# Attention and two MLPs on one core: transfers counted at 270 GB/s in a planner, softmax normalisation of two blocks also on ScalarE, table changes by rank

## The chip, the cores and the metric

The kernel runs on one core of a Trainium2 chip. The metric is device microseconds of one execution. Engines carry the names of the profile: PE is TensorE, PEld its weight loads, DVE is VectorE, ACT is ScalarE, POOL is GpSimd, SP is SyncE, whose instructions only issue DMAs here.

## What is computed

Chunked attention (4 sequences, 8 heads, 768 tokens, head size 64; chunks of 32 queries see 16 keys to the left, 8 to the right and 8 memory tokens), then two MLPs over the 3072 tokens (512 to 2048 to 512). The weights are 64-bit floats in memory.

```python
def _attn_ref(q, k, v, mem_k, mem_v):
    chunk, left_ctx, right_ctx = (32, 16, 8)
    scale = 1.0 / np.sqrt(D)
    for c in range(S // chunk):
        c_start, c_end = c * chunk, c * chunk + chunk
        l_start, r_end = max(0, c_start - left_ctx), min(S, c_end + right_ctx)
        k_full = np.concatenate([mem_k, k[:, :, l_start:r_end]], axis=2)
        v_full = np.concatenate([mem_v, v[:, :, l_start:r_end]], axis=2)
        scores = scale * np.matmul(q[:, :, c_start:c_end], k_full.transpose(0, 1, 3, 2))
        a = np.exp(scores - np.max(scores, axis=-1, keepdims=True))
        a = a / (np.sum(a, axis=-1, keepdims=True) + 1e-09)
        out[:, :, c_start:c_end] = np.matmul(a, v_full)

# x: the attention's output as 3072 rows of 512
h = x @ w_in;  x = (h * np.tanh(np.log1p(np.exp(h)))) @ w_out        # first MLP (Mish)
h = x @ w2_in; x = (h * (1.0 / (1.0 + np.exp(-1.702 * h)))) @ w2_out  # second MLP
```

## The kernel before

**Tiles and stages.** The tokens are cut into 8 blocks of 384. Each block needs 8 quads of attention (a quad is two heads by 192 tokens) and 16 steps of the first MLP (a step is one slice of 128 of the 2048 hidden columns). The second MLP follows over pairs of blocks, in 32 units with seven products each. Matmuls with fp32 accuracy are made of three in fp32r: a value is split into a rounded part (xh, gh) and a remainder (xl, gl). The attention of block 0 runs alone at the start, that of block j+1 between the steps of block j, so the quads of block 1 lie among the steps of block 0.

**One quad.** For blocks 0 and 1 the heads are turned on PE (L673, bank `h`) and copied out of PSUM by ACT (L680) or DVE (L681) into qT or kT. Scores run on PE (L708, banks s0, s1 and, in block 0, o0, o1), DVE takes the row minimum with the mask (L721), ACT takes the exponentials e and their sums sm (L736, four pieces), DVE makes the sums' reciprocals r (L754, L758) and multiplies e by them (L761). PE turns e (L782), ACT or DVE copies it into aT (L788, L789), PE multiplies by the values vt (L799 in block 0, L808 behind it), and ACT or DVE rounds the result into xh (L834, L836; two halves in blocks 1 and on), DVE makes xl (L840).

**One step.** PE runs twelve matmuls into a bank `h` (L895), ACT applies Mish (L907, into buffers gh and gl in turn in block 0), PE multiplies by the output weights into four banks that are held through the block (L924), which leave through ACT (L951) or DVE (L954). There are two banks `h`, shared by the turning of heads and the steps: a step can't begin before the copy L680 or L681 has emptied its bank.

**Weights.** In block 0 each step's weights are loaded as words of 64 bits (wi, wo, 512 KB each, L299) and made into fp32 by one scaling on ACT or DVE (L343, L346) and three operations on DVE (L352, L356, L360), then split (L378 on ACT or L379 on DVE, L384); those of wo are stored to DRAM for later (w1d).

**What sets the order.** Every piece of work is an operation with a rank (its place in an ideal order; a quad takes 2 ranks, a step 1) and one or more ways, each an engine with an estimated duration. `Plan.issue()` plays these through once when the program is built: whenever an engine is free, it takes the ready operation of the lowest rank. A second way is taken if its engine would be ready sooner than the queue of the first. ACT needs a table for exponentials and another for Mish, and an operation of the other table is taken only if nothing else is ready. A transfer is issued by SP in that order and is thought to land after the transfers before it, at a rate that `bus()` gives, plus a lag. The outcome is a fixed order of instructions on each engine, in which every one waits for its data in place. A planner's number therefore never changes how long an instruction takes; it changes which instruction stands in front of which.

`load` hands each transfer to SP with that time:

```python
size = bus(nbytes / len(parts), run)
ways = [("sp", 0.475, lambda go=go: go(nc.sync), size), ...]
```

Of the kernel before, what the change touches and what calls it, by code (L numbers as in the profile page):

```python
# [81 lines left out]
class Plan:  # L82
# [2 lines left out]

    LAG = {"pe": 0.2, "act": 0.16, "dve": 0.13, "pool": 0.2}
    RELOAD = 1.4

    def __init__(self):
        self.ops = []  # L90

    def add(self, rank, ways, reads=(), writes=(), updates=(), chain=None, table=None):
        op = Op()
        op.table = table
        op.rank, op.ways, op.seq = rank, ways, len(self.ops)
        op.after, op.at = [], 0.0
        need = {}

        def wait(o, lag=True):
            need[id(o)] = (o, lag or need.get(id(o), (o, False))[1])  # L100

        for b in (*reads, *updates):
            for o in b.writers:
                wait(o)
        for b in (*writes, *updates):
            for o in b.readers:
                wait(o)
            b = b.whole
            if not b.users and b.tag is not None:
                made = b.tag.made  # L110
                k = made.index(b)
                if k >= b.tag.bufs:
                    b.gate += [(o, True) for o in made[k - b.tag.bufs].users]
                    made[k - b.tag.bufs].closed = True
                if k:
                    b.gate.append((made[k - 1].users[0], False))
        for b in writes:
            for o, lag in b.whole.gate:
                wait(o, lag)
        for b in updates:  # L120
            b.writers, b.readers = [], []
        for b in (*writes, *updates):
            b.writers.append(op)
        for b in reads:
            b.readers.append(op)
        for b in (*reads, *writes, *updates):
            assert not b.whole.closed
            b.whole.users.append(op)
        if chain is not None:
            if chain:  # L130
                wait(chain[-1], False)
            chain.append(op)
        op.need = len(need)
        for o, lag in need.values():
            o.after.append((op, lag))
        self.ops.append(op)
        return op

    def issue(self):
        engines = ("pe", "act", "dve", "pool", "sp")  # L140
        free = dict.fromkeys(engines, 0.0)
        ready = {e: [] for e in engines}
        load = dict.fromkeys(engines, 0.0)
        coming = []
        bus = 0.0
        for op in self.ops:
            if op.need == 0:
                heapq.heappush(coming, (0.0, op.seq, op))
            op.start = None
        left = len(self.ops)  # L150
        now = 0.0
        table = None
        order = []
        while left:
            while coming and coming[0][0] <= now + 1e-9:
                op = heapq.heappop(coming)[2]
                for w, (e, dur, *_) in enumerate(op.ways):
                    heapq.heappush(ready[e], (op.rank, op.seq, w, op))
                load[op.ways[0][0]] += op.ways[0][1]
            for e in engines:  # L160
                if free[e] > now + 1e-9:
                    continue
                kept = []
                pick = other = None
                while ready[e]:
                    item = heapq.heappop(ready[e])
                    op, w = item[3], item[2]
                    if op.start is not None:
                        continue
                    if w:  # L170

                        e0, d0 = op.ways[0][:2]
                        if max(free[e0] - now, 0.0) + load[e0] - d0 < op.ways[w][1] - d0 + 0.3:
                            kept.append(item)
                            continue
                    if e == "act" and op.table not in (None, table):

                        if other is None:
                            other = item
                        else:  # L180
                            kept.append(item)
                        continue
                    pick = item
                    break
                if pick is None:
                    pick = other
                elif other is not None:
                    kept.append(other)
                for item in kept:
                    heapq.heappush(ready[e], item)  # L190
                if pick is None:
                    continue
                op, w = pick[3], pick[2]
                e_, dur, fn, *size = op.ways[w]
                op.start, op.way = now, w
                load[op.ways[0][0]] -= op.ways[0][1]
                order.append(op)
                left -= 1
                end = now + dur
                if e == "act" and op.table not in (None, table):  # L200
                    if table is not None:
                        end += self.RELOAD
                    table = op.table
                free[e] = end
                lag = self.LAG.get(e, 0.0)
                if size:
                    bus = max(bus, end + 0.65) + size[0]
                    end, lag = bus, 0.9
                for o, far in op.after:
                    t = end + lag if far else (now + 0.01 if not size else now + 0.01)  # L210
                    o.at = max(o.at, t)
                    o.need -= 1
                    if o.need == 0:
                        heapq.heappush(coming, (o.at, o.seq, o))
            times = [coming[0][0]] if coming else []
            times += [free[e] for e in engines if free[e] > now + 1e-9]
            if not times:
                assert not left, "operations wait for one another"
                break
            now = min(t for t in times if t > now) if any(t > now for t in times) else now  # L220
        order.sort(key=lambda o: (o.start, o.seq))
        for op in order:
            op.ways[op.way][2]()


def dve(n, fast=False):
    return (170 + (0.53 if fast else 1.04) * n) / 1000


def act(n, psum=False):  # L230
    return ((180 if psum else 220) + 0.86 * n) / 1000


def bus(nbytes, run):
    return nbytes / 360e3 * (1 if run >= 512 else 2)


@with_exitstack
def kernel(
# [449 lines left out]
    def quad(j, hp, gp, heads, rank):  # L689
# [74 lines left out]

        add(rank + 1.4, [("dve", 0.23, plus)], reads=[sm], writes=[r])
        add(rank + 1.4, [("dve", 0.16, inverse)], updates=[r])
        add(rank + 1.4, [("dve", dve(4 * P), norm)], reads=[r, done], updates=[e])

        return after, e

# [484 lines left out]
```

## Time and profile before

| | us |
|---|---|
| median of 3 runs | 1215.35 (1214.6 to 1215.85) |
| the profiled execution's own time | 1215.45 |
| its span, first to last instruction | 1213.3 |
| PE busy in the span | 1183.9 (98%) |
| DVE busy | 822.5 (68%) |
| ACT busy | 564.9 (47%) |
| POOL busy | 10.1 (1%) |

The profile is of one execution. Its span is 2.15 us shorter than its own time, which holds the launch as well, and its own time is 0.1 us above the median of the runs. The busy time of an engine is the sum of its instructions; an engine that waits in place for data is idle in it. Matmuls are pipelined, and a busy PE can run at either of two levels of its clock, which the profile gives as the granted share of full speed.

### The profile page before, as it was taken

How to read it: one execution, taken by the hardware profiler on the slowest of the kernel's cores; microseconds unless marked ns; L12 is line 12 of the kernel's file. 1: busy time of each engine (PE TensorE's matmuls, PEld its weight loads, DVE VectorE, ACT ScalarE, POOL GpSimd, SP SyncE). 2: the span in 40 equal slices, each digit the busy share in tenths (PEclk: the TensorE clock that was granted, in tenths of full speed). 3: DMA queues.
4: the chain of work that ended last, by engine and by line, in shares of the span. 5: the costliest groups of instructions: out<-in, count | busy, mean ns of one | idle time of the engine just before them, and what ended most of it. 6: DMA issues, size and time to landing. Idle time of an engine off the chain costs nothing.

```text
span 1213.3 us, 19142 instructions
## 1 busy us (share of the span) xinstructions
PE 1183.9 (98%) x6656; PEld 1082.8 (89%) x6656; DVE 822.5 (68%) x2379; ACT 564.9 (47%) x1303; POOL 10.1 (1%) x27
## 2 busy tenths in 40 slices
PE   7689999999999999999999999999999999999998
PEld 6567789999999999999999998998889888988897
DVE  5798878776866767667665668877655855555554
ACT  4677666655555555655533344445212521232112
POOL 1000000000000000000000000000000000000000
PEclk8799999999999999999999999999999999999999
DMA  9965545533433333334212676699656865566521
GB/s 204 262 216 168 147 124 139 147 94 80 114 88 92 98 91 93 103 81 116 60 49 74 229 257 209 231 356 335 214 186 194 296 226 189 179 224 214 181 106 53
DMA packets 214687, 197.80 MB, mean 163 GB/s; under 512 B 133496, under 2 KB 176519, under 8 KB 214591
## 3 DMA queue, kind: packets, MB, share of 16 engines
q1 hardware_dynamic: 214239, 195.82, 53.0%
q0 software_dynamic: 352, 0.75, 0.4%
q8 instruction: 53, 0.87, 0.3%
q14 instruction: 43, 0.35, 0.1%
HBM read 148.29 MB, written 48.23 MB: 162 GB/s over the span
## 4 chain that ended last, share of the span: by engine, by line
PE 93%; DMA 3%; SPq 2%; DVE 1%; ACT 1%; issue 0%; ACTq 0%
PE h L895 22%; PE o L924 22%; PE h L1057 19%; PE o L1084 15%; PE s L1084 7%; PE s L808 3%; PE s L708 3%; SPq L299 2%; PE s L782 2%; DMA vt<-in_v_dram 1%; DMA wo<-in_moe_w_out_dram 0%; DMA wi<-in_q_dram 0%; DMA x1d<-ev 0%; DMA st<-w1d 0%; DMA w1d<-u 0%
## 5 line engine op out<-in xcount | busy, mean ns | idle before, releaser
L895 PE MATMUL h<-xh,wi 128*128 128x384 f32 x1024 | 269.0, 344 | 5.9 <-ACT qT L680 4.4
L924 PE MATMUL o<-gh,wo 128*128 128x384 f32 x896 | 240.6, 349 | 0.0
L895 PEld LDWEIGHTS h<-xh,wi 128*128 128x128 f32 x1024 | 184.3, 189 | 13.2 <-ACT qT L680 5.2
L895 PE MATMUL h<-xl,wi 128*128 128x384 f32 x512 | 172.9, 338 | 0.0
L924 PEld LDWEIGHTS o<-gh,wo 128*128 128x128 f32 x896 | 158.0, 188 | 2.8
L924 PE MATMUL o<-gl,wo 128*128 128x384 f32 x448 | 150.8, 337 | 0.0
L907 ACT ACTIVATE u<-h 128x384 f32<-128x384 f32 x112 | 55.0, 491 | 132.0 <-PE h L895 125.5
L736 ACT ACTIVATE e<-e,mx 96x128 f32<-96x128 f32 x240 | 94.0, 393 | 23.5 <-DVE mx L721 22.9
L944 DVE TENSOR_TENSOR gl<-u,gh 128x384 fp32r<-128x384 f32 x177 | 96.9, 554 | 11.4 <-ACT gh L939 8.6
L895 PEld LDWEIGHTS h<-xl,wi 128*128 128x128 f32 x512 | 96.7, 189 | 0.0
L1057 PE MATMUL h<-wi,wi 128*128 128x384 f32 x480 | 94.4, 337 | 0.0
L1057 PEld LDWEIGHTS h<-wi,wi 128*128 128x128 f32 x480 | 85.5, 188 | 4.9 <-ACT v L1124 0.2
L924 PEld LDWEIGHTS o<-gl,wo 128*128 128x128 f32 x448 | 84.1, 188 | 0.0
L1124 ACT ACTIVATE v<-h 128x384 f32<-128x384 f32 x61 | 29.9, 490 | 113.2 <-PE h L1057 113.2
L1084 PE MATMUL o<-wo,gh 128*128 128x512 f32 x262 | 82.1, 394 | 0.2 <-ACT ev L951 0.2
L721 DVE CUSTOM_DVE_ANT_0 e<-s,mask 96x128 f32<-96x128 f32 x240 | 55.7, 283 | 37.5 <-PE s L708 36.4
L1057 PE MATMUL h<-wo,wi 128*128 128x384 f32 x384 | 77.2, 336 | 0.0
L907 ACT ACT_TABLE_LOAD x55 | 70.6, 1283 | 10.6 <-PE h L895 9.9
L1107 ACT ACTIVATE u<-e 128x384 f32<-128x384 f32 x64 | 33.5, 524 | 85.2 <-DVE e L1130 85.1
L736 ACT ACT_TABLE_LOAD x54 | 69.3, 1283 | 6.7 <-DVE mx L721 5.8
L1057 PEld LDWEIGHTS h<-wo,wi 128*128 128x128 f32 x384 | 68.2, 188 | 3.0 <-DVE u L1109 0.2
L836 DVE CAST xh<-s 64x192 fp32r<-64x192 f32 x84 | 29.8, 355 | 50.9 <-PE s L808 41.6
(195 smaller groups left out, 2057.8 us busy)
## 6 DMA issues: line engine op xcount, KB each, us to landing
wi<-w2c SPq DMA_DIRECT2D x72, 512.0 KB
wo<-w2o SPq DMA_DIRECT2D x48, 512.0 KB
w2c<-wi SPq DMA_DIRECT2D x24, 512.0 KB
st<-x1d SPq DMA_DIRECT2D x56, 192.0 KB
wi<-in_moe_w_in_dram SPq DMA_DIRECT2D x16, 512.0 KB
wo<-in_moe_w_out_dram SPq DMA_DIRECT2D x16, 512.0 KB
st<-in_moe_w_in_dram SPq DMA_DIRECT2D x16, 512.0 KB
w2d<-v SPq DMA_DIRECT2D x32, 256.0 KB
```

Source lines behind the costliest of these rows:

```text
L708: nc.tensor.matmul(out=s[hh][:, i, :], lhsT=queries(d, i), rhs=keys(d, i), start=True, stop=True,)
L721: nc.vector.tensor_tensor_reduce(out=e[:, i, hh, :], in0=s[hh][:, i, :], in1=mask[:GQ, mask_of(g0 + i), :], scale=-scale, scalar=-NEG, op0 ...
L736: nc.scalar.activation(out=e[:, i, hh, :], in_=e[:, i, hh, :], func=AF.Exp, scale=-1.0, bias=mx[:, i, hh:hh + 1], accum_out=sm[:, i, hh:hh ...
L808: nc.tensor.matmul(out=o[:, i].rearrange("p h t -> p (h t)"), lhsT=vt[:, g + i, h:h + 2].rearrange("p h d -> p (h d)"), rhs=aT[:, i].rearr ...
L895: nc.tensor.matmul(out=h.get(), lhsT=a[:, c], rhs=b[:, kk, :], start=(n == 0), stop=(n == 3 * KD - 1))
L907: add(i + 0.3, [("act", act(TB, True), lambda: nc.scalar.activation(out=u.get(), in_=h.get(), func=AF.Mish))], reads=[h], writes=[u], tabl ...
L924: nc.tensor.matmul(out=o.get(), lhsT=a[:, c], rhs=b.get(), start=(first and n == 0), stop=(last and n == len(prods) - 1),)
L944: add(rank + 0.05, [("dve", dve(TB), lambda: nc.vector.tensor_tensor(out=gl.get(), in0=u.get(), in1=gh.get(), op=ALU.subtract))], reads=[u ...
L1057: nc.tensor.matmul(out=bank.get(), lhsT=a, rhs=b, start=(fresh and m == 0), stop=(m == 3 * K2 - 1), skip_group_check=not fresh,)
L1084: nc.tensor.matmul(out=o.get(), lhsT=a[:, c], rhs=w[:, b:b + DM], start=(first and k == 0), stop=(last and k == 2))
L1107: add(rank, [("act", act(TB, True), lambda: nc.scalar.activation(out=u.get(), in_=src(), func=AF.Tanh, scale=0.851))], reads=[src.buf], wr ...
L1124: ("act", act(TB, True), lambda: nc.scalar.activation(out=dst.get(), in_=bank.get(), func=AF.Copy)),
```

## The change

Three things are changed in the planner and one in the kernel. First, `bus()` counts transfers at 270 GB/s in place of 360, and multiplies by 1.5 for runs of 256 to 511 bytes and by 2.5 below (2 for both before); the fixed parts around a transfer go from 0.65 and 0.9 us to 0.9 and 1.1. Second, an ACT operation that needs the other table is now also taken while others are ready, if its rank is lower than theirs by more than PATIENCE = 1.0. Third, the multiplication of e by the reciprocals has a second way for blocks 0 and 1 (EARLY = 2): four ACT copies with a scale, `norm_act`. Everything else of the kernel's text stands.

```diff
@@ class Plan
     RELOAD = 1.4
+    PATIENCE = 1.0
@@ def issue(self)
-                if pick is None:
-                    pick = other
-                elif other is not None:
+                if other is not None and (pick is None or other[0] + self.PATIENCE < pick[0]):
+                    pick, other = other, pick
+                if other is not None:
                     kept.append(other)
@@
                 if size:
-                    bus = max(bus, end + 0.65) + size[0]
-                    end, lag = bus, 0.9
+                    bus = max(bus, end + 0.9) + size[0]
+                    end, lag = bus, 1.1
@@ def bus(nbytes, run)
-    return nbytes / 360e3 * (1 if run >= 512 else 2)
+    return nbytes / 270e3 * (1 if run >= 512 else 1.5 if run >= 256 else 2.5)
@@ def quad
         add(rank + 1.4, [("dve", 0.16, inverse)], updates=[r])
-        add(rank + 1.4, [("dve", dve(4 * P), norm)], reads=[r, done], updates=[e])
+        def norm_act():
+            for i in range(2):
+                for hh in range(2):
+                    nc.scalar.activation(
+                        out=e[:, i, hh, :], in_=e[:, i, hh, :], func=AF.Copy, scale=r[:, i, hh, :]
+                    )
+
+        ways = [("dve", dve(4 * P), norm), ("act", 4 * act(P), norm_act)]
+        add(rank + 1.4, ways if j < EARLY else ways[:1], reads=[r, done], updates=[e])
```

Lines from L86 on move down by one, and those behind `quad` by nine: L299 becomes L300, L680 is L681, L788 is L797, L834 is L843, L907 is L916; the new pieces are L771. In all, 5 of the normalisations of blocks 0 and 1 go from DVE to ACT (20 pieces). Of the scalings 3 go from ACT to DVE, of the roundings of weights 4 from DVE to ACT, of the bank copies 3 from ACT to DVE, of the roundings into xh and of the copies into aT one each, and 4 output copies go from DVE to ACT. ACT loads a table 111 times in both.

SP, around the first value loads of block 1 (vt from in_v_dram and in_mem_v_dram; wi3 is a 512 KB weight load for step 3), before:

```order
L544 DMA ql_157<-in_mem_k_dram 8x4x32 x4
L299 DMA wi3_400<-in_moe_w_in_dram 128x4x256
L299 DMA vt_412<-in_v_dram 120x8x64
L299 DMA vt_412<-in_mem_v_dram 8x8x64
L299 DMA vt_412<-in_v_dram 120x8x64
L299 DMA vt_412<-in_mem_v_dram 8x8x64
L299 DMA wi4_570<-in_moe_w_in_dram 128x4x256
```

and after:

```order
L545 DMA ql_149<-in_mem_k_dram 8x4x32 x4
L300 DMA vt_444<-in_v_dram 120x8x64
L300 DMA vt_444<-in_mem_v_dram 8x8x64
L300 DMA vt_444<-in_v_dram 120x8x64
L300 DMA vt_444<-in_mem_v_dram 8x8x64
L300 DMA wi3_528<-in_moe_w_in_dram 128x4x256
L300 DMA wi4_567<-in_moe_w_in_dram 128x4x256
```

The load for step 3 stands behind the four value loads now.

ACT, in front of the first Mish of the program (xh_623 is the xh of block 1, qT_645 the copy that empties the bank of step 0), before:

```order
L788 ACTIVATE aT_609<-s0_602 128x384
L736 ACTIVATE e_572,sm_600<-e_572,mx_573 96x128 x3
L834 ACTIVATE xh_623<-s1_618 64x192 x2
L343 ACTIVATE v_630<-wi2_212 128x512
L343 ACTIVATE u_634<-wo1_215 128x512
L343 ACTIVATE st_639<-wi3_400 128x512
L680 ACTIVATE qT_645<-h_500 128x448
L343 ACTIVATE u_650<-wo2_225 128x512
L343 ACTIVATE v_666<-wi4_570 128x512
L907 ACT_TABLE_LOAD
L907 ACTIVATE gh_683<-h_653 128x384
```

and after (qT_633 is that copy):

```order
L771 ACTIVATE e_495<-e_495,r_569 96x128 x4
L344 ACTIVATE v_603<-wi2_203 128x512
L344 ACTIVATE u_614<-wo1_214 128x512
L737 ACTIVATE e_585,sm_621<-e_585,mx_586 96x128 x4
L681 ACTIVATE qT_633<-h_499 128x448
L344 ACTIVATE u_641<-wo2_217 128x512
L379 ACTIVATE wi1_657<-st_557 128x512
L771 ACTIVATE e_585<-e_585,r_635 96x128 x4
L344 ACTIVATE st_671<-wi3_528 128x512
L916 ACT_TABLE_LOAD
L916 ACTIVATE gh_676<-h_644 128x384
```

No L843 (the former L834) of block 1 stands ahead of the copy any more; of the five moved normalisations one stands here ahead of it (another further up, in block 0) and one between it and the Mish.

PE, in the attention of block 0 (wi13 and wo13 hold q and k of its second half of tokens here), before:

```order
L708 MATMUL o1_219<-qT_204 96x128
L782 MATMUL o2_249<-ident_67,e_167 128x96 x4
L673 MATMUL h_260<-ident_67,wi13_126 128x96
L673 MATMUL h_260<-ident_67,wo13_121 128x128
L673 MATMUL h_260<-ident_67,wi13_126 128x96
L673 MATMUL h_260<-ident_67,wo13_121 128x128
L673 MATMUL h_267<-ident_67,wi13_126 128x96
L673 MATMUL h_267<-ident_67,wo13_121 128x128
L673 MATMUL h_267<-ident_67,wi13_126 128x96
L673 MATMUL h_267<-ident_67,wo13_121 128x128
L799 MATMUL o3_279<-aT_265,vt_114 64x96 x4
```

and after:

```order
L709 MATMUL o1_221<-qT_206 96x128
L674 MATMUL h_254<-ident_67,wi13_126 128x96
L674 MATMUL h_254<-ident_67,wo13_121 128x128
L674 MATMUL h_254<-ident_67,wi13_126 128x96
L674 MATMUL h_254<-ident_67,wo13_121 128x128
L674 MATMUL h_261<-ident_67,wi13_126 128x96
L674 MATMUL h_261<-ident_67,wo13_121 128x128
L674 MATMUL h_261<-ident_67,wi13_126 128x96
L674 MATMUL h_261<-ident_67,wo13_121 128x128
L791 MATMUL o2_270<-ident_67,e_169 128x96 x4
```

The turning of the weights e of the first quad (L782, now L791) moved behind the eight transposes of the second half.

## Rows read from the trace of the kernel before

**Rows 1.** The page: the span, and busy time and instructions of each engine.

```profile
span 1213.3 us, 19142 instructions
PE 1183.9 (98%) x6656; PEld 1082.8 (89%) x6656; DVE 822.5 (68%) x2379; ACT 564.9 (47%) x1303; POOL 10.1 (1%) x27
```

**Rows 2.** Stretches: length, busy us of PE PEld DVE ACT POOL, clock, DMA, GB/s.

```profile
0.00:10.00 10.00, 6.58 (x38) 6.15 (x39) 1.32 (x11) 1.28 (x1) 5.99 (x14) 1.00 0.93 153
10.00:42.00 32.00, 24.76 (x228) 19.29 (x227) 26.99 (x135) 22.44 (x91) 0.00 (x0) 0.80 0.97 214
42.00:51.20 9.20, 2.45 (x7) 1.17 (x6) 5.99 (x15) 4.57 (x14) 0.00 (x0) 0.50 1.17 262
51.20:57.50 6.30, 5.61 (x24) 4.86 (x25) 2.52 (x9) 3.50 (x6) 0.00 (x0) 0.59 1.08 348
57.50:102.50 45.00, 39.02 (x207) 29.99 (x205) 41.27 (x111) 33.75 (x74) 0.00 (x0) 1.00 0.71 232
102.50:145.50 43.00, 43.00 (x214) 33.19 (x213) 36.37 (x106) 25.66 (x56) 0.21 (x1) 1.00 0.45 130
145.50:1190.00 1044.50, 1043.27 (x5862) 972.06 (x5861) 699.10 (x1979) 468.91 (x1057) 3.92 (x12) 1.00 0.52 160
1190.00:1213.30 23.30, 19.19 (x90) 16.05 (x88) 8.93 (x18) 4.84 (x9) 0.00 (x0) 1.00 0.18 69
```

**Rows 3.** The chain of waits in order of time: start, us, what.

```profile
41.26 5.86 DMA vt<-in_v_dram
...
47.16 1.02 PE s L808 x2
...
51.29 4.21 PE h L895 x12
...
90.03 4.95 DMA wo<-in_moe_w_out_dram
...
102.59 2.29 PE h L895 x12
```

**Rows 4.** ACT in time: start, us, instruction; in brackets its wait and releaser.

```profile
48.21 0.66 ACT L834 ACTIVATE xh<-s 64x192 fp32r<-64x192 f32 x2 [4.01 <-PE s L808]
48.90 0.66 ACT L343 ACTIVATE v<-wi 128x512 f32<-128x512 f32 x1
...
50.70 0.54 ACT L680 ACTIVATE qT<-h 128x448 f32<-128x448 f32 x1
```

**Rows 5.** SP's queue in time, at the value loads of block 1.

```profile
39.78 0.40 SPq L299 DMA_DIRECT2D wi<-in_moe_w_in_dram  x1
40.35 0.37 SPq L299 DMA_DIRECT2D vt<-in_v_dram  x1
```

**Rows 6.** PE in time, its waits between 57.5 and 102.5.

```profile
65.65 0.62 PE L895 MATMUL h<-xh,wi 128*128 128x384 f32 x2 [1.42 <-ACT gl L907]
...
88.53 2.85 PE L924 MATMUL o<-gh,u 128*128 128x384 f32 x8 [3.24 <-ACT gh L907]
...
99.61 0.61 PE L895 MATMUL h<-xh,wi 128*128 128x384 f32 x2 [1.32 <-ACT qT L680]
```

**Rows 7.** ACT in time, the two L834 ahead of those waits.

```profile
85.33 0.66 ACT L834 ACTIVATE xh<-s 64x192 fp32r<-64x192 f32 x2 [1.02 <-PE s L808]
...
98.33 0.66 ACT L834 ACTIVATE xh<-s 64x192 fp32r<-64x192 f32 x2 [2.18 <-PE s L808]
```

**Rows 8.** Groups by line: busy us, mean ns, then idle ahead and its cause.

```profile
L736 ACT ACTIVATE e<-e,mx 96x128 f32<-96x128 f32 x240 | 94.0, 393 | 23.5 <-DVE mx L721 22.9
L761 DVE TENSOR_TENSOR e<-e,r 96x512 f32<-96x512 f32 x60 | 41.1, 685 | 1.2
L836 DVE CAST xh<-s 64x192 fp32r<-64x192 f32 x84 | 29.8, 355 | 50.9 <-PE s L808 41.6 <-ACT xh L834 7.6
```

**Rows 9.** Waits of ACT from 40 to 103: us, count, longest.

```profile
ACT xh L834 <- PE s L808: 7.2, 3, 4.0
```

**Rows 10.** PE in time, at the first L782 of block 0.

```profile
16.19 0.52 PE L782 MATMUL o<-ident,e 96*128 96x96 f32 x4 [1.25 <-ACT e L736]
...
17.38 0.27 PE L673 MATMUL h<-ident,wi 96*128 96x96 f32 x1 [0.67 <-DMA wi<-in_q_dram]
```

## The prediction

> **What bounds the kernel now.** I read the page first: TensorE's matmuls fill 98% of the span, 1183.9 of 1213.3 us [rows 1]. The next question is where the other 29.4 us are, so I cut the span into stages [rows 2]. From 145.5 to 1190 us the PE is busy for 1043.27 of 1044.5 us at full clock, and from 102.5 to 145.5 for all of 43.00. The tail from 1190 on holds 4.1 us without a matmul (23.3 less 19.19): the last outputs leaving. The first 10 us hold 3.4 us in which the first loads land. What is left lies between 10 and 102.5 us: 7.2 (32 less 24.76), 6.75 (9.2 less 2.45), 0.7 and 5.98 us (45 less 39.02). [...] So a change of order can win only here, in attention of block 0 and the first nine steps of the first MLP, and can lose anywhere.
>
> Two waits make most of it. *First jam.* The chain of waits [rows 3] goes: a load of values (vt) issued at 41.26 lands at 47.12, L808 (weights times values, first quad of block 1) runs, then ACT's L834, three conversions L343, the bank copy L680, and only then at 51.29 the first step of the MLP (L895, step 0). ACT's own rows [rows 4] say why: ACT stood 4.01 us in front of L834, waiting for L808, and the copy at 50.70 that frees the PSUM bank of step 0 was queued behind it. SP's rows [rows 5] show a 512 KB weight load (wi) issued at 39.78, right in front of the values. *Second jam.* Of the 5.98 us after 57.5, PE waits 3.24 us at 88.53 for gh, 1.32 at 99.61 for a bank copy and 1.42 at 65.65 [rows 6]. In front of the first two, ACT again stood at L834 for L808: 1.02 us before 85.33 and 2.18 before 98.33 [rows 7].
>
> **The change, part by part.**
>
> *A. Values ahead of the weight load; L834 on DVE.* In SP's new order the 512 KB load stands behind the four value loads. It took 0.57 us of SP's time (39.78 to 40.35 [rows 5]) and at the 262 GB/s of the stretch in which it lands [rows 2] 524 KB take 2.0 us of transfer; the values land between 0.57 and 2.0 us sooner. I take 2.0, since the DMA engines were full there (share 1.17): 45.1 instead of 47.1. The second L808 takes 1.02, so PE is done with it at 46.2. The bank: in the new order no L834 of block 1 stands ahead of the copy (qT) on ACT. I counted what does. Before: 40 exponentials, 7 bank copies, 5 L788, 6 L834, 6 L343. After: 40, 4, 5, 5, 4, and 8 pieces of the moved normalisation. Less are 3 copies of 0.54, 1 L834 of 0.33 (0.66 for two) and 2 L343 of 0.66 [rows 4], 3.3 us; more are 8 pieces. A piece is a 96x128 activation, like the exponentials at 393 ns [rows 8]: 3.1 us. So ACT has the same work ahead of the copy, without the wait of 4.01: the copy ends at 51.24 less 4.0, 47.2, and step 0 begins there. Term A: **-4.1 us** (51.29 to 47.2). Ends: -5.1 if only L808 holds it (46.2), -2.1 if ACT waits elsewhere for half of the 4.01.
>
> *B. Steps 1 to 8.* From step 0 to step 8 the old order has L834 on ACT three times (six pieces; waits of 7.2 us in all [rows 9], of which 4.01 is the first jam), the new one once (one piece, the other half on DVE). Counting PE's rows up to step 8, both orders hold 8 steps and 24 L924, so like is compared with like. Of 3.24 and 1.32 I leave one of the smaller size, 1.3, since the chain reaches 99.61 by a weight load of 4.95 us (wo, [rows 3]) that the new order holds too, and keep the 1.42, whose row is a table load in front of gl that stands in the new order too. Term B: **-3.3 us** (4.56 less 1.3). Ends: 0 (jams elsewhere) and -5.98 (none left). What is late next is DVE: it was busy for 5.99 + 2.52 + 41.27 = 49.8 of the 60.5 us from 42 to 102.5 [rows 2]. The new order takes 3 normalisations of 685 ns off it there [rows 8] and gives it 5 pieces of L836 at 355 ns [rows 8], so its work is unchanged, and 60.5 less 7.4 leaves 53.1 us: 94% busy. It ran at 92% from 57.5 to 102.5, so that is near its limit but within it; A and B together can't pass 10.7.
>
> *C. Attention of block 0.* PE's new order puts the transposes of the second half of the tokens ahead of the first L782. They waited for q until 17.38, while the first L782 ran at 16.19 [rows 10]: eight of them take 0.8 us, so that L782 moves to 18.2, 2.0 us later, and the score work behind it sooner. DVE is 84% busy there (26.99 of 32), and one normalisation and one copy leave its queue in the meantime. Price between -1 (the freed DVE time) and +2.0; I take **+0.4**, near nothing, as DVE and not the order of PE sets that stage's end.
>
> *D. The rest.* PE holds the same instructions in both orders, and from its second third on the two differ by a place here and there. PE is full there, so what feeds it is ahead of it. Four output copies (L954) go from DVE to ACT (L951), busy for only 469 of those 1044.5 us [rows 2]. Table loads: 111 in both orders, so the new rule by rank moves some and saves none. Cost 0; ends +1.2 and -1.2, the 1.23 us that PE was idle there.
>
> Sum: -4.1 - 3.3 + 0.4 = -7.0 us. The profiled execution took 1215.45 us, 2.15 outside its span, 0.1 above the median of 1215.35. Forecast 1215.45 - 7.0 = **1208.4 us**.
>
> **The rivals.**
>
> *The clock stays up, or the jams all go.* Step 0 took 4.21 us at the lower level and a later step 2.29 [rows 3]. PE was idle for 6.75 us between 42 and 51.2. Idle shrinks to about 4 us in the new order. If the level stays high, PE's 5.61 us from 51.2 to 57.5 at 0.59 become 3.3, and the L808 half a microsecond shorter: 2.8 more. Or B reaches -5.98, 2.7 more. Either gives 1205.6, both up to DVE's limit 1204.7 (-10.7). For it: DVE has just the room. Against: PE still stands from about 42 to 45 waiting for values, and the level had fallen by 42 already. Chance 0.22. [...]
>
> *Nothing measurable.* Values land only 0.57 sooner, ACT finds another wait before the copy (-2.1), steps 1 to 8 keep their jams (0), block 0's attention ends 1 us later: -1.1, 1214.3. For it: DVE at 92% means that any engine's lead is soon given back. Against: the chain names one removable wait of 4.01. Chance 0.15.
>
> *Slower: ACT waits for reciprocals instead.* The new pieces of normalisation (four, in ACT's order) stand in front of gh of step 0, of step 4 and of step 8, and each waits for L758 in DVE's full queue. If DVE brings the reciprocal later than ACT's own work and a step of PE (2.29) cover, ACT stands there as it did at L834, and PE waits for gh as at 88.53: three places at 3.24 are 9.7 us, -7.0 + 9.7 = +2.7, **1218.2**. It decides from a lag of about 2.3 us on. For it: one such place is on ACT just ahead of the first gh. Against: in DVE's order the reciprocal stands two rows behind L754, which reads the sums, and a row there takes at most 0.7 us. Chance 0.13.
>
> That the planner's numbers change and the order hardly does is excluded by the orders themselves.
>
> **How the numbers follow.** Forecast 0.50, better by the clock or the jams 0.22, nothing 0.15, slower 0.13. What can be told from no change is about 0.2%, 2.4 us: 1212.9 to 1217.8. Faster holds the first two, 0.72; same 0.15; slower 0.13. The sum's own ends are -5.1 - 5.98 - 1 - 1.2 = -13.3 and -2.1 + 2.0 + 1.2 = +1.1. The range 1203 to 1215.5 leaves out the slower case and a twentieth below.
>
> **What would show it.** Right: step 0 of L895 begins near 47 us, and step 8 near 95 (102.5 before); no ACT wait of 4 us at L834; PE idle between 57.5 and step 8 at 2 to 3 us; from there on PE full, the rest of the span as long as before. Wrong: step 0 at 50 or later (values or the bank); a wait of ACT at the normalisation for L758; PE idle rows after 145 us of more than 2 us; or PE's first L782 of block 0 setting the end of its attention later than 43 us.

## The result: 1.05% faster, nearly twice the forecast

| | before | changed |
|---|---|---|
| median | 1215.51 us (4 runs, 1214.6 to 1215.85) | 1202.74 us (4 runs, 1201.15 to 1203.97) |
| ratio | | 0.9895, 95% interval 0.9878 to 0.9913 |
| measured again, beside other kernels | 1216.03 us | 1202.03 us, 0.9885, interval 0.987 to 0.99 |

The forecast was 1208.4 us in a range from 1203.0 to 1215.5: the sign and the place were right, the size was not (12.8 us in place of 7.0), and the time lies just below the range. The page of the changed kernel, which answers to [rows 1]:

```profile
span 1200.7 us, 19141 instructions
PE 1181.3 (98%) x6656; PEld 1081.9 (90%) x6656; DVE 820.0 (68%) x2373; ACT 567.6 (47%) x1324; POOL 10.0 (1%) x27
```

The span is 12.6 us shorter. PE's work went from 1183.9 to 1181.3 us, its idle time from 29.4 to 19.4. Cut at the first matmul of step 0 and of step 8 (L895, in the changed kernel L904), the columns as in [rows 2], before:

```profile
0.00:51.29 51.29, 33.79 (x268) 26.61 (x268) 34.40 (x160) 28.38 (x106) 5.99 (x14) 0.78 1.00 211
51.29:102.52 51.23, 44.65 (x229) 34.85 (x229) 43.72 (x119) 37.18 (x79) 0.00 (x0) 0.95 0.76 246
102.52:1213.30 1110.78, 1105.45 (x6162) 1021.30 (x6160) 744.38 (x2102) 499.38 (x1120) 4.13 (x13) 1.00 0.51 157
```

and changed:

```profile
0.00:45.98 45.98, 32.40 (x269) 26.04 (x269) 31.20 (x153) 28.06 (x109) 5.99 (x14) 0.81 0.96 201
45.98:89.68 43.70, 42.49 (x223) 33.74 (x221) 41.70 (x115) 36.47 (x80) 0.00 (x0) 0.97 0.93 294
89.68:1200.70 1111.02, 1106.43 (x6170) 1022.10 (x6168) 747.16 (x2107) 503.08 (x1137) 3.99 (x13) 1.00 0.51 158
```

So 5.3 us came before step 0, 7.5 between step 0 and step 8, and the remaining 1111 us are as long as before (+0.2). Of the 7.5, 5.4 are idle time of PE (6.58 to 1.21) and 2.2 are PE's own work: one quad's scores (8 matmuls, 0.6 us) now stand behind step 8, and the mean clock of the stretch is 0.97 in place of 0.95. The 5.3 divide in the same way: 3.9 are idle time (17.50 to 13.58) and 1.4 are PE's own work, with nearly the same matmuls (268 and 269) at a mean clock of 0.81 in place of 0.78. So about 3 us of the gain, in these two executions, are the same work of PE done faster, and not waits. The stretches of [rows 2] show when the lower level, 0.50, ended:

```profile
42.00:51.20 9.20, 7.03 (x32) 5.52 (x32) 8.22 (x22) 7.73 (x21) 0.00 (x0) 0.64 1.13 269
51.20:57.50 6.30, 5.99 (x33) 4.93 (x32) 6.25 (x19) 5.90 (x13) 0.00 (x0) 1.00 1.07 350
57.50:102.50 45.00, 44.10 (x231) 34.57 (x230) 42.14 (x115) 36.81 (x82) 0.00 (x0) 1.00 0.78 256
```

From 51.2 to 57.5 the clock was 0.59 before and is 1.00 now. The traces of these two executions hold only the clocks 0.50 and 1.00, and a figure between them is a mean over a change: from 0.50 to 1.00 at 56.42 us before and at 48.60 now. The chain of waits, against [rows 3], runs from the value loads straight to step 0:

```profile
41.16 4.16 DMA vt<-in_mem_v_dram
...
45.45 0.98 PE s L817 x2
46.43 3.15 PE h L904 x12
```

and the bank copy, last to end in [rows 4], had ended at 44.0 us, 2.0 us before step 0 began:

```profile
43.49 0.52 ACT L681 ACTIVATE qT<-h 128x448 f32<-128x448 f32 x1
```

Of the waits in [rows 6] two small ones are left:

```profile
56.82 0.61 PE L904 MATMUL h<-xh,wi 128*128 128x384 f32 x2 [0.32 <-ACT gl L916]
...
81.12 0.62 PE L904 MATMUL h<-xh,wi 128*128 128x384 f32 x2 [0.90 <-ACT gl L916]
```

In all tables below "step 0" and "step 8" are the starts of these steps in the profiled execution, and ratios are against the kernel before on the same chip. Executions of one kernel differ: the kernel before took 1212.98 to 1219.61 us in 20 runs on one chip.

### The profile page after: what moved, and what is told of

Read it like the earlier page. It is cut to its first block, busy times and chain, and to the rows that moved or that the text cites. A ratio compares the mean times of both kernels' runs of the same rounds, so it can differ in the third digit from the quotient of the medians.

```text
span 1200.7 us, 19141 instructions
## 1 busy us (share of the span) xinstructions
PE 1181.3 (98%) x6656; PEld 1081.9 (90%) x6656; DVE 820.0 (68%) x2373; ACT 567.6 (47%) x1324; POOL 10.0 (1%) x27
## 4 chain that ended last, share of the span: by engine, by line
PE 94%; SPq 2%; DVE 1%; DMA 1%; ACT 1%; issue 0%; ACTq 0%
PE h L904 22%; PE o L933 22%; PE h L1066 20%; PE o L1093 15%; PE s L1093 7%; PE s L817 3%; PE s L709 3%; SPq L300 2%; PE s L791 1%; DMA vt<-in_v_dram 1%; DMA vt<-in_mem_v_dram 0%; ACT e L737 0%; ACT L737 0%; DVE wi L385 0%; ACT L916 0%
## 5 line engine op out<-in xcount | busy, mean ns | idle before, releaser
L904 PE MATMUL h<-xh,wi 128*128 128x384 f32 x1024 | 269.7, 344 | 2.1 <-ACT gl L916 1.2
L904 PEld LDWEIGHTS h<-xh,wi 128*128 128x128 f32 x1024 | 184.2, 189 | 10.5 <-ACT gl L916 1.6
L904 PE MATMUL h<-xl,wi 128*128 128x384 f32 x512 | 172.5, 337 | 0.0
L916 ACT ACTIVATE u<-h 128x384 f32<-128x384 f32 x112 | 55.0, 491 | 137.0 <-PE h L904 128.6
L953 DVE TENSOR_TENSOR gl<-u,gh 128x384 fp32r<-128x384 f32 x177 | 97.2, 554 | 12.6 <-ACT gh L948 9.4
L904 PEld LDWEIGHTS h<-xl,wi 128*128 128x128 f32 x512 | 96.5, 188 | 0.0
L845 DVE CAST xh<-s 64x192 fp32r<-64x192 f32 x86 | 30.5, 355 | 48.1 <-PE s L817 37.8
```

The source lines that it names most:

```text
L845: nc.vector.tensor_copy(out=x, in_=y)
L904: nc.tensor.matmul(out=h.get(), lhsT=a[:, c], rhs=b[:, kk, :], start=(n == 0), stop=(n == 3 * KD - 1))
L916: add(i + 0.3, [("act", act(TB, True), lambda: nc.scalar.activation(out=u.get(), in_=h.get(), func=AF.Mish))], reads=[h], writes=[u], tabl ...
L953: add(rank + 0.05, [("dve", dve(TB), lambda: nc.vector.tensor_tensor(out=gl.get(), in0=u.get(), in1=gh.get(), op=ALU.subtract))], reads=[u ...
```

## Experiments: the three parts apart

Three switches on the changed kernel undo one part each; every single part and every pair was run.

```diff
 # table changes by rank off
-    PATIENCE = 1.0
+    PATIENCE = 1e9
 # transfer numbers as before
-    return nbytes / 270e3 * (1 if run >= 512 else 1.5 if run >= 256 else 2.5)
+    return nbytes / 360e3 * (1 if run >= 512 else 2)
-    bus = max(bus, end + 0.9) + size[0];  end, lag = bus, 1.1
+    bus = max(bus, end + 0.65) + size[0]; end, lag = bus, 0.9
 # normalisation on VectorE alone
-    add(rank + 1.4, ways if j < EARLY else ways[:1], reads=[r, done], updates=[e])
+    add(rank + 1.4, ways if j < 0 else ways[:1], reads=[r, done], updates=[e])
```

**norm_only** (tables and transfers undone):

> Only the second way of the normalisation (ScalarE, blocks 0 and 1); transfers counted as before, no table change by rank. In the order of this kernel the value loads of block 1 already stand ahead of the 512 KB load, and no rounding into xh of block 1 stands ahead of the bank copy of step 0. Theory 1 (this part moves the loads and the queue of ScalarE, and with them the first jam): step 0 begins near 46 us (45.98 in the changed kernel, 51.29 before), which is 5.3 us, and the time is 1206 to 1211. Theory 2 (the transfer numbers make the gain): step 0 after 49 us and the time within 2.4 us of before. Theory 3 (table changes by rank make it): step 0 near 46 but no gain in steps 1 to 8, 1210.

**bus_only** (tables and normalisation undone):

> Only the transfer numbers (270 GB/s, factors for short runs, the two fixed parts). In the order of this kernel the 512 KB load still stands ahead of the values, but the rounding into xh of block 1 stands behind the bank copy of step 0. Theory 1: the values land at 47 us as before and step 0 waits for L817 and not for the copy, so it begins near 48.2, 3 us earlier; steps 1 to 8 keep their jams; the time is 1211 to 1214. Theory 2 (the transfer numbers make the gain): step 0 near 46 and the time 1204 to 1208. Theory 3: within 2.4 us of before.

**table_only** (transfers and normalisation undone):

> Only the table changes by rank. The order up to the first Mish is that of before, so step 0 begins at 51.3 us in every theory. Up to the eighth Mish ScalarE holds 6 roundings into xh in place of 10. Theory 1 (the normalisation makes the gain): time within 2.4 us of before. Theory 3 (a table change that comes earlier ends the waits for gh at step 4 and for the bank at step 7, 3.24 and 1.32 us): 1209 to 1212, and step 8 at 96 to 99 us in place of 102.5.

**no_norm**:

> The changed kernel without the second way of the normalisation (transfer numbers and table changes by rank stay). Its order has the value loads behind the 512 KB load and the rounding into xh of block 1 behind the bank copy. Theory 1: it loses most of the gain, 1210 to 1214, with step 0 near 48.2 us. Theory 2 or 3 (the other two parts make the gain): 1203 to 1207.

**no_bus**:

> The changed kernel with the old transfer numbers (normalisation on ScalarE and table changes by rank stay). Its order has the value loads ahead of the 512 KB load, and the scaling of that load's words (L344, st) ahead of the bank copy of step 0, as in the kernel with the normalisation alone, where ScalarE stood 3.37 us there. If the parts need each other: the same wait of 3 to 4 us at L344 for the weight load, step 0 near 47.3 us, and a time of 1208 to 1211. If the parts just add up (2.4 and 1.8 us): 1210.9 as well, but without that wait and with step 0 near 46. If the transfer numbers do nothing here: 1202 to 1204.

**no_table**:

> The changed kernel without table changes by rank. Its order is that of the changed kernel up to the first Mish, so step 0 begins at 46.0 us by every theory. If table changes by rank end waits for Mish in steps 1 to 8 (as the wait of 1.01 us before step 2 in the kernel with the transfer numbers alone, gone with the rule), step 8 comes 1 to 3 us later than 89.7 and the time is 1204 to 1206. If VectorE alone bounds steps 0 to 8 (it was busy 41.70 of 43.70 us in the changed kernel), the time is within 1 us of 1202.7, since this kernel moves more normalisations to ScalarE by the eighth Mish (24 pieces against 16).

| kernel | ratio, interval | step 0 | step 8 | between |
|---|---|---|---|---|
| before | 1 | 51.29 | 102.52 | 51.23 |
| table_only | 0.9982 (0.9971 to 0.9992) | 51.81 | 102.06 | 50.25 |
| norm_only | 0.998 (0.9964 to 0.9995) | 47.26 | 101.94 | 54.68 |
| bus_only | 0.9941 (0.9922 to 0.9961) | 47.61 | 97.81 | 50.20 |
| no_bus | 0.9947 (0.993 to 0.9964) | 48.32 | 94.87 | 46.55 |
| no_norm | 0.9932 (0.9909 to 0.9954) | 47.44 | 96.16 | 48.72 |
| no_table | 0.9914 (0.9896 to 0.9933) | 44.79 | 92.28 | 47.49 |
| changed | 0.9895 (0.9878 to 0.9913) | 45.98 | 89.68 | 43.70 |

Theory 1, that the normalisation makes the gain, fell: by the ratios it brings 2.4 us alone, the transfer numbers 7.2 and the table rule 2.2. Together that is 11.8, the whole gain within the intervals. Theory 2 named the largest part, and it too was wrong to expect all of it from there. Theory 3 fell with table_only, whose step 8 came at 102.06 and not at 96 to 99 us. The pairs agree: the transfer numbers cost most when they are undone (no_bus), the table rule least (no_table, 1204.29 us with step 8 2.6 us later, as the first theory of its expectation had it; its interval overlaps that of the changed kernel). The forecast had not said which part does what. In these orders the value loads come ahead of the 512 KB load where the normalisation has its second way (norm_only, no_bus, no_table), whatever the transfer numbers. With the old transfer numbers, the scaling of that load's words (L344) stands ahead of the bank copy, and ScalarE waits there for the load; norm_only's ScalarE in time:

```profile
46.11 0.66 ACT L344 ACTIVATE st<-wi 128x512 f32<-128x512 f32 x1 [3.37 <-DMA wi<-in_moe_w_in_dram]
46.67 0.53 ACT L681 ACTIVATE qT<-h 128x448 f32<-128x448 f32 x1
```

One wait had taken the place of another, as the pair without the transfer numbers confirms (no_bus, ScalarE's waits from 40 to 103 us: total, times, longest):

```profile
ACT st L344 <- DMA wi<-in_moe_w_in_dram: 6.6, 2, 4.2
```

Earlier table changes shorten the stretch between the steps much only with the normalisation on ScalarE: 47.49 to 43.70 us with the new transfer numbers, 54.68 to 46.55 with the old, of which a part is the clock (norm_only's profiled execution took 1216.55 us, 4 more than its median, and the mean clock of its stretch was 0.86, against 0.93 in no_bus). Without it the stretch shrinks by 1.0 and 1.5. In the times this is not clear of noise: the rule brings 2.3 and 4.0 us with the normalisation, 2.2 and 1.1 without, by the ratios.

## Experiments: single instructions moved

Here the planner's order is kept and instructions are moved by hand in it, with a few lines behind the planner. Operation 237 is the bank copy of step 0, 213 the first rounding into xh of block 1, 347 the 512 KB load, 366 the load after the values.

**copy_first**, on the kernel before:

```diff
-        order.sort(key=lambda o: (o.start, o.seq))
+        order = moved(sorted(order, key=lambda o: (o.start, o.seq)))
+def moved(order):
+    # take operation 237 out and put it in front of 213
```

> The kernel before, with one instruction moved: the bank copy of step 0 (L680, qT) stands ahead of the two L834 of block 1 in ScalarE's order, nothing else. Theory of the first jam: step 0 then waits for the second L808 alone and begins at 48.2 us in place of 51.29 (47.16 + 1.02), 3.1 us, and the time falls by about that, to 1211 to 1213. Rival (the head start is given back in steps 1 to 8, VectorE being full): step 8 stays near 102.5 and the time within 1 us of before.

**copy_and_values_first**, the same and:

```diff
+    # take operation 347 out and put it in front of 366, behind the values
```

> The kernel before with that move and one more: the 512 KB weight load stands behind the four value loads of block 1 in SP's order. Theory of the first jam: the values land about 2 us sooner and step 0 begins near 46.0 us, as in the changed kernel (45.98), 5.3 us before 51.29, of which this second move brings 2; the time is 1208.5 to 1210.5. What is left to the changed kernel's 1202.7, 6 to 8 us, then belongs to steps 1 to 8. Rival (the order of the loads changes nothing, since all transfers share the same engines): step 0 stays at 48.2.

Step 0 came as early as expected, or earlier (46.75 and 45.91 us), and neither time fell: 1.0004 (0.9992 to 1.0016) and 1.0009 (0.9996 to 1.0022). The whole head start was given back by step 8 (102.63 and 105.23). In copy_first the stretch between the steps grew by 4.65 us, 2.5 of them idle time of PE and 2.1 PE's own work:

```profile
46.75:102.63 55.88, 46.77 (x230) 36.20 (x229) 46.13 (x124) 39.66 (x84) 0.00 (x0) 0.92 0.77 243
64.00:66.00 2.00, 2.00 (x8) 2.00 (x7) 2.00 (x8) 0.00 (x0) 0.00 (x0) 0.50 0.95 329
88.00:90.00 2.00, 2.00 (x5) 1.08 (x4) 2.00 (x4) 0.08 (x1) 0.00 (x0) 0.50 1.13 313
```

The idle time: ScalarE now reached the scaling of the next weights before they had landed, the copies behind it came late, and PE waited 2.26 us for a Mish ahead of step 2 where it had waited 1.42 [rows 6]:

```profile
53.96 0.68 ACT L343 ACTIVATE st<-wi 128x512 f32<-128x512 f32 x1 [1.27 <-DMA wi<-in_moe_w_in_dram]
62.79 0.94 PE L895 MATMUL h<-xh,wi 128*128 128x384 f32 x2 [2.26 <-ACT gl L907]
87.20 4.32 PE L924 MATMUL o<-gh,u 128*128 128x384 f32 x8 [3.23 <-ACT gh L907]
```

PE's own work: the clock was 0.50 behind that wait, and again behind the wait of 3.23 us for gh, which is 3.24 in [rows 6]. In the kernel before it stayed up behind the same wait:

```profile
88.00:90.00 2.00, 1.47 (x5) 0.94 (x6) 1.97 (x5) 1.43 (x3) 0.00 (x0) 1.00 0.95 270
```

In copy_and_values_first the stretch grew by 8.1 us. ScalarE stood 3.8 us in front of a scaling for its load, and PE 3.24 behind it:

```profile
ACT st L343 <- DMA wi<-in_moe_w_in_dram: 3.8, 1, 3.8
57.03 1.33 PE L808 MATMUL s<-aT,vt 128*128 128x192 f32 x3 [3.24 <-ACT aT L788]
```

Of the 8.1 us, 3.8 are idle time of PE (10.37 in place of 6.58) and 4.3 PE's own work (48.95 in place of 44.65), at a mean clock of 0.88 in place of 0.95. So about half of each head start went into new waits, which begin where an instruction that was moved ahead meets a load still on its way, and half into the clock.

**values_before_keys**, on the changed kernel, since step 0 there waits for the values, and SP had eight small loads of keys ahead of them:

```diff
+    # take operations 503 to 506 and 494 to 497 (kl, ql of block 2) out, put them in front of 347
```

> The changed kernel with one move in SP's order: the eight small loads of keys for block 2 (kl x4, ql x4, 35.05 to 39.75 us on SP) stand behind the four value loads of block 1 and no longer ahead. The values then are issued at 35.1 in place of 39.9 and land near 40.5 in place of 45.3, and step 0 waits for the bank copy that ended at 44.0. Theory of the values: step 0 near 44, 2 us earlier. Of the time: 1200 to 1201.5 if the rest of the order follows; 1202 to 1204 if the head start is given back as in the two kernels with moved instructions on the order of before.

Step 0 came at 43.16 us, step 8 at 87.91, 1.8 us before the changed kernel's, and the head start held to step 24 (175.44 against 176.99). The time was the changed kernel's all the same: 0.9888 (0.9873 to 0.9903). Behind step 24 PE was busy without a gap in both, but the matmuls of L904 on xh took longer, 343 ns against 340 in the changed kernel, from 240 to 640 us:

```profile
L904 PE MATMUL h<-xh,wi 128*128 128x384 f32 x632 | 165.4, 343 | 0.0
```

From step 32 to step 127 the two kernels differ by 2.0 us (470.3 and 468.3), and what made these matmuls slower no run here shows.

## Experiments: other rates in the planner

**rate_240** and **rate_310**, the changed kernel with one number:

```diff
-    return nbytes / 270e3 * (...)
+    return nbytes / 240e3 * (...)   # the other: 310e3
```

> The changed kernel with 240 GB/s in the planner in place of 270. If the gain comes from an order in which no engine stands in front of a load that is still on its way, a slower rate keeps that property (the scaling of the third load, L344 st, stands behind the first Mish here) and the time is 1200 to 1206, with no wait of ScalarE for a weight load over 1 us up to step 8. If 270 is a lucky draw among orders, the time is anywhere from 1200 to 1215.

> The changed kernel with 310 GB/s in the planner in place of 270. In its order the scaling of the third load (L344, st) stands ahead of the bank copy of step 0 again, as at 360. If ScalarE's standing in front of loads is the price: a wait of 2 to 4 us at L344 for the weight load, step 0 near 48 us and a time of 1206 to 1210. If 270 is a lucky draw among orders: anywhere from 1200 to 1215, without such a wait going with the slow ones.

They came to 0.994 (0.9925 to 0.9955) and 0.9914 (0.9897 to 0.9931): both better than before and both worse than 270, by 7 and 4 us in the medians beside norm_back_in_place below, on the same chip. The reason that I had given for the slow ones was wrong. In rate_310 ScalarE waits for no weight load; step 0 came at 51.68 us behind a chain of VectorE's work, and the steps after it were quick (42.15 us to step 8). In rate_240 step 0 came at 41.59 us, 4.4 before the changed kernel's, and step 8 at 89.77 as in the changed kernel. This head start, too, was gone by step 8, and nearly all of it in PE's own work: 46.30 us in place of 42.49, at a clock of 0.90 in place of 0.97.

```profile
41.59:89.77 48.18, 46.30 (x224) 37.50 (x225) 41.98 (x117) 34.62 (x73) 0.00 (x0) 0.90 0.91 271
```

Rate_240's loss of 5.5 us in the span lies in the second MLP. Three of the 5.5 are waits of PE between 800 and 900 us. The mean clock was 0.98 in that stretch, and 1.00 from 700 to 800 and from 900 to 1000 us, which adds to the loss. The waits:

```profile
PE h L1066 <- ACT xl L1041: 2.0, 1, 2.0
PE h L1066 <- DVE wi L434: 0.8, 1, 0.8
```

So an order within a few us of the best is a draw: small changes of a planner's number move the time by up to 7 us, and 270 is a good draw, not a proof that the transfers run at that rate. The sizes of the three parts above are sizes of such draws as well.

## Experiments: which engine is full

**norm_back_in_place**, the order of the changed kernel, three normalisations on the other engine:

```diff
+    at[209].way = at[247].way = at[333].way = 0   # VectorE
```

> The changed kernel with its order kept instruction for instruction; only the three normalisations that stand on ScalarE behind step 0 (12 pieces, 4 in front of the first Mish) run on VectorE at the same places of the order. If VectorE bounds steps 0 to 8 (busy 41.70 of 43.70 us in the changed kernel), two of them fall into that stretch and cost 2 x 0.685 us there: step 8 about 1.4 us later, time 1203.5 to 1205. If the gain of the normalisation lies in the order that the planner made with it and not in VectorE's time: no difference within 1 us. If ScalarE is the tighter engine (four pieces took 1.26 us there): up to 1 us faster.

**dve_twice** and **act_twice**, the order of the changed kernel, six operations issued twice:

```diff
+    for n in (350, 319, 407, 376, 414, 433):   # L357; act_twice: (367, 405, 355, 424, 462, 374), L344
+        at[n].ways[at[n].way] = the same, with its instruction issued twice
```

> The changed kernel with its order kept, and six operations of VectorE on weight words (L357, 0.69 us each, two OR's of the same bits give the same) issued twice between steps 1 and 8: 4.1 us more work on VectorE. If VectorE bounds steps 0 to 8 (41.70 of 43.70 us busy): step 8 comes 2 to 4.1 us later and the time rises by that, to 1205 to 1207 on a chip where the changed kernel takes 1202.7. If it doesn't: less than 1 us.

> The changed kernel with its order kept, and six scalings of ScalarE (L344, 0.66 us each) issued twice between steps 1 and 5: 4.0 us more work on ScalarE, which was busy 36.47 of 43.70 us there. If VectorE is the bound: less than 1 us, as ScalarE has 7 us to spare. If ScalarE's queue is what PE waits for (PE's two waits of 0.32 and 0.90 us in that stretch end with a Mish on ScalarE): 2 to 4 us more, 1205 to 1207.

**xh_on_scalar**, six roundings into xh on ScalarE at the same places:

```diff
+    for n in (232, 234, 251, 253, 280, 282): at[n].way = 0   # ScalarE
```

> The changed kernel with its order kept, and six roundings into xh of block 1 (three pairs, in steps 2 to 6) on ScalarE in place of VectorE at the same places. Theory of the jam, as in the forecast: ScalarE stands for L817 in front of them, 1 to 2 us each time, with a Mish queued behind, and the time rises by 2 to 5 us. If VectorE bounds the stretch: it gets 6 x 0.355 = 2.1 us off and the time falls by 1 to 2 us. If neither: within 1 us.

**after_again**:

> The changed kernel itself, beside the others on the same chip: 0.9895 of before by the first measurement (0.9878 to 0.9913).

**before_dve_twice**, the edit of dve_twice on the kernel before:

> The kernel before with its order kept, and the same six operations of VectorE on weight words (L356 here, 4.1 us in all) issued twice. If the price of the kernel before was the order (engines standing for one another) and VectorE had 7.5 us to spare in steps 0 to 8: the time rises by less than 2 us, against 4 in the changed kernel. If VectorE's work bounds both kernels: by 4 us as there.

| kernel | median, us | ratio, interval | step 0 to 8 |
|---|---|---|---|
| after_again | 1202.03 | 0.9885 (0.987 to 0.99) | 44.04 |
| act_twice | 1202.89 | 0.9892 (0.9877 to 0.9906) | 45.31 |
| xh_on_scalar | 1205.56 | 0.9913 (0.9898 to 0.9929) | 46.05 |
| dve_twice | 1206.12 | 0.992 (0.9904 to 0.9937) | 46.17 |
| norm_back_in_place (another chip) | 1203.11 | 0.9883 (0.9868 to 0.9897) | 45.23 |
| before_dve_twice (another chip) | 1216.88 | 1.0005 (0.9991 to 1.0019) | 51.75 |

The first four ran on one chip. By the medians, four us more on VectorE cost 4.1 us and four more on ScalarE 0.9, which is not clear of noise. The same four on VectorE of the kernel before cost 0.6 by the ratio and 1.3 by the medians, not clear of noise either. So work added on VectorE at these six places delays the changed kernel, while in the kernel before VectorE had room for it, which fits a price that lay in the order. The rows of the stretch say the same, VectorE's busy time being the third, in after_again and dve_twice, and then in before_dve_twice:

```profile
46.13:90.17 44.04, 42.83 (x223) 34.08 (x221) 41.58 (x114) 36.26 (x79) 0.00 (x0) 0.96 0.94 291
45.94:92.11 46.17, 43.57 (x223) 33.47 (x221) 44.80 (x119) 34.79 (x74) 0.00 (x0) 0.98 0.90 280
```

```profile
51.61:103.36 51.75, 45.26 (x228) 34.99 (x228) 46.98 (x124) 37.61 (x79) 0.00 (x0) 0.95 0.76 245
```

Only 2.1 of dve_twice's 4.1 us show in the profiled executions (spans of 1203.2 and 1201.2 us): that of dve_twice was the fastest of its four runs, that of after_again the slowest. norm_back_in_place speaks neither for this nor against it: of its three normalisations one fell into the stretch (0.69 us), and no changed kernel ran beside it. That VectorE alone sets the pace is not shown. PE itself is busy for 42.49 of the 43.70 us in the changed kernel, and the next two kernels, which take work off VectorE, gain nothing.

xh_on_scalar brings the jam of the forecast back by itself. VectorE had 2 us less to do, and the time rose by 3.5 us in the medians (the intervals touch). ScalarE stood in front of the roundings for L817 (1.7 us), and PE for the Mish behind them, 3.4 us against 1.2 in after_again (the last line):

```profile
ACT xh L843 <- PE s L817: 1.7, 2, 1.1
```

```profile
PE h L904 <- ACT gl L916: 3.4, 3, 1.9
```

```profile
PE h L904 <- ACT gl L916: 1.2, 2, 0.9
```

**values_first_norms_scalar**, a version that was meant to be better than the changed kernel: values_before_keys and

```diff
+    at[228].way = at[276].way = 1   # two more normalisations on ScalarE
```

> The changed kernel with the key loads of block 2 behind the value loads of block 1 (step 0 at 43.2 us in place of 46 in the run that had this alone), and the two normalisations that VectorE still has in steps 1 to 8 on ScalarE at the same places (1.4 us off VectorE, 2.5 us more on ScalarE, which took 4 us more without harm over 1 us). If VectorE bounds the stretch: step 8 at 86 to 87 and a time 1 to 3 us under the changed kernel, a ratio of 0.986 to 0.988. If the head start is given back: 0.988 to 0.990, the same as the changed kernel.

Step 0 at 42.80 and step 8 at 87.65 us, yet 0.9898 (0.988 to 0.9915): no better than the changed kernel, and no better than values_before_keys, with the same slow matmuls of L904 (343 ns). VectorE was busy for 1 us less between the steps (42.27 and 43.22 us), and step 8 came 0.3 us sooner.

## Why the prediction was wrong, step by step

- **What bounds the kernel: right.** All of the gain lies ahead of step 8, and the rest of the span is 0.2 us longer.
- **A, the first jam: near in size (5.3 us, against 4.1, or 3.7 with the 0.4 of C), wrong as a price of its own.** The values landed at 45.31 us (45.1 forecast), L817 ended at 46.4 (46.2). The error was the copy: I let it end at 47.2 with ScalarE's work as before, it ended at 44.0, so the upper end of the step (46.2) came true. 1.4 of the 5.3 us are PE's own work, which the term did not hold. And the step took the jam for a price of its own: copy_first and copy_and_values_first bring step 0 as early in the order of before and gain nothing, and rate_240 brings it 4.4 us earlier still and has step 8 no sooner.
- **B, steps 1 to 8: the step that failed, 7.5 us against 3.3.** The term was 4.56 less 1.3: I counted two waits (3.24 and 1.32), left one of 1.3 and kept the 1.42 whole, 2.7 us of jams. In the runs 5.4 us of PE's idle time went and 1.21 are left. The other 2.2 us are PE's own work, for which the sum held nothing: 0.6 are the scores that moved behind step 8, and most of the rest is the clock (a mean of 0.97 in place of 0.95), which I had put among the rivals. The range then ended at 1203.0, though the sum's own ends reached to -13.3, 1202.2.
- **VectorE's limit: wrong by its count.** I had "its work is unchanged" from 42 us on, and from that a bound of 10.7 us for A and B together. VectorE's busy time from 42 us to step 8 fell from 49.8 to 45.3 us. The three normalisations less were right, and four L845 came in place of five. What I had not counted are four roundings of weights (L379) that went to ScalarE, although they stand in the list of the change, five subtractions (L849) less, and the operations on words of two weight pieces, which were put off behind step 8. That more work on VectorE would cost time next was right, as dve_twice shows.
- **C, attention of block 0: right in its rows.** The first L791 ran at 18.32 us (18.2 forecast). Its price can't be told apart within the 5.3 us.
- **D: right here (+0.2), but no law.** rate_240 lost 5.5 us of its gain in the second MLP.
- **The rivals.** The one that came true is the first, "the clock stays up, or the jams all go": both happened in part, the clock rising at 48.60 us in place of 56.42. Its price for both together, 1204.7 us at VectorE's limit, was still 2 us too high. PE's idle time from 42 to 51.2 us went from 6.75 to 2.17 us; that less idle time is what raised the clock sooner was my guess, and no run shows it. The rise came in stretches in which PE was busy for 7.03 of 9.20 us (changed) and 5.61 of 6.30 (before). The fall can't be read from the length of a wait alone: after waits of 3.23 and 3.24 us the clock was 0.50 in one kernel and 1.00 in the other. Nor did it fall in the long idle stretch behind 42 us: in the kernel before it fell at 39.36 us, among waits of PE of 0.6 to 1.0 us. The rival of the reciprocals stayed small (ScalarE waited 0.8 us at L771).
- What stays open: which of the many places in the order make the 7.5 us. The parts add up and were not traced to single instructions, the clock's share is read from single executions, and the slower matmuls of L904 have no known cause.

## What to carry to other kernels

A wait on the chain is worth its length only if what comes next is not late too: in a fixed order of several engines fed by loads, a head start of 4.5 us, won by moving one copy, was gone eight steps later, half of it in new waits and half in the clock, while three mild changes of the planner, which re-time everything, won 12.8. Count PE's own work beside its waits: about 3 of these 12.8 us are the same work done at a higher clock. To see which engine has room left, issue an operation twice on one engine and then on another, in the unchanged order; here that cost 4.1 us on VectorE and 0.9 on ScalarE. And when a planner's number is tuned, run its neighbours: 240 and 310 differed from 270 by several us, and not for the reason that I had expected.

## What the runs showed of the chip that I had not expected

- The same wait of PE, 3.23 and 3.24 us, ended with the clock at 0.50 in copy_first and at 1.00 in the kernel before.
- Of norm_only's ten executions the slower ones had the lower mean clock: the five up to 1212.54 us 0.990 or 0.991, the five from 1212.74 us 0.987 or 0.988. The fastest took 1209.85 us at 0.990, the slowest 1218.03 at 0.987. That difference in the clock is worth some 4 of the 8 us, an estimate from the share of the span that was not granted.
- Matmuls of one line, of the same shape and at a clock of 1.00, from 240 to 640 us, had a mean of 340 ns in the changed kernel and 343 in the two kernels in which the key loads had been moved behind the value loads.
